# Retention followed by a soft mixture of experts: step 18's keys turned on the chip, one unit of token products held back, the last write in halves

## The chip, the cores and the metric

One Trainium2 chip, one of its cores. The metric is the device time of one execution in microseconds (us), the median of the runs shown. A unit of time in the profile is a us from the start of the profiled span unless it says ns.

## The reference, cut to what matters

```
def _attn_ref(q, k, v):                       # (4, 8, 768, 64) each
    gamma = 1.0 - 2.0 ** (-5.0 - arange(H)); scale = 1.0 / sqrt(D)
    for t in range(S):
        state = gamma * state + einsum('bhd,bhe->bhde', k[:, :, t], v[:, :, t])
        y[:, :, t] = scale * einsum('bhd,bhde->bhe', q[:, :, t], state)

def _moe_ref(x, phi, w1, w2):                 # x (3072, 512), w1 (8, 512, 1024), w2 (8, 1024, 512)
    logits = x @ phi                          # 32 slots, 4 to an expert
    d = softmax(logits over tokens);  slot_input = d.T @ x
    for e in range(E): slot_out[e] = relu(slot_input[e] @ w1[e]) @ w2[e]
    c = softmax(logits over slots);   return c @ slot_out
```

`x` is `y` with its heads beside each other: 4 sequences of 768 tokens, 512 columns.

## The kernel before, in words

Everything is float32. The tokens are cut into 24 **steps** of 128 (4 sequences by 6 chunks, the sequence running fastest), and the steps go in pairs through a loop `for P in range(NPP)` (L451). For each step PE makes scores (`score_mm`, L227), DVE masks them (L235), PE adds the carried state's part and the masked part (L251, L260), sums keys times values into the state (`state_mm`, L288), turns the result back to tokens by rows (`natural_mm`, L304), and the router's logits and dispatch sums follow in groups of four steps. After the loop come two products with the expert weights: `hidden` (L589) with `w1`, and the product with `w2` (L669) in three blocks of output columns, `BLOCKS` = 256, 128 and 128 wide.

**Inputs.** A step's input tile has four parts of 512 columns: keys transposed, queries transposed, values, and the keys once more by tokens (`kn`), which `state_mm` wants as its stationary operand. A step in `TURNED` (L46), and the last four, is "lean": its load (`load_in`, L199) brings 1536 columns, 768 KB, and for a step in `TURNED` PE turns the keys itself (`turn_k`, L206: four 128x128 transposes into a PSUM bank, and one copy by ACT, L207). Any other step loads 2048 columns, 1024 KB (L201). Step `i` is loaded in the iteration `P = (i - 6) / 2` and, when turned, is turned in `P = (i - 2) / 2`, just ahead of that iteration's `natural_mm`. The expert weights are 1 MB tiles (L163, L166) and half tiles (L181), interleaved with the input loads by the table `PACE`.

**Order of the work.** The engines' instructions stand in the order in which the program writes them. All loads and all writes of the output are issued by SP, one queue, in program order, and each has its packets spread over the core's 16 DMA engines, which work through them in that order.

**The end.** When a block's `w2` product is complete in its bank, the generator `finish` (L630) does three things: DVE copies the sums out (`os`, L634); PE repeats the 32 slots over the partitions (`rep`, L638) and DVE copies that (`s4`, L639); then per unit `(m, h)`, 128 output columns by half of the tokens, four **token products** (L650) go into four PSUM banks, are copied by DVE (j even) and ACT (j odd) into an output tile (L655), and SP writes the tile, 768 KB (L656). Blocks 0 and 1 interleave their `finish` with the next block's `w2` product; block 2's has nothing behind it. There are eight units, so eight writes: four of block 0, two of block 1, two of block 2. `rep` is a matrix that repeats the slots; `cT` holds the combine weights; `r` are the ring's 1024-column slots; `b` the 2048-column tiles.

Of the kernel before, what the change touches and what calls it, by code (L numbers as in the profile page):

```python
# [16 lines left out]
B, H, S, D = 4, 8, 768, 64  # L17
C = 128
# [17 lines left out]
BLOCKS = [(0, 256), (256, 128), (384, 128)]  # L36
Y1 = (3, 3, 1)
# [5 lines left out]
NIN = 6  # L43
NRING = 9
PACE = (1, 1, 1, 2, 1, 2, 1, 2, 2, 0, 2, 2)
TURNED = (0, 1, 2, 3, 4, 8, 12, 14)  # L46
SIW = 48
LEAN = [i for i in range(1, NSTEP) if i in TURNED or i >= NSTEP - B]
FULL = [i for i in range(1, NSTEP) if i not in LEAN]
# [32 lines left out]
def retention_soft_moe_kernel(  # L82
# [9 lines left out]
    nc = tc.nc  # L92
# [6 lines left out]
    big = ctx.enter_context(tc.tile_pool(name="big", bufs=NBIG))  # L99
# [18 lines left out]
    rep = small("rep", [128, 128])  # L118
# [7 lines left out]
    cT = small("cT", [128, NGRP, C])  # L126
# [324 lines left out]
    for P in range(NPP):  # L451
        last = P == NPP - 1
# [45 lines left out]
        if P < NPP - B // 2:  # L498
            state_mm(P)
            state_add(P)  # L500
        if 2 * P + 2 in TURNED:
            turn_k(2 * P + 2, "A0")
# [66 lines left out]
    for k in range(NK):  # L569
        nc.tensor.matmul(sp[:, k, :], acc[:, k * 128:(k + 1) * 128], wsel, start=True, stop=True,  # L570
                         skip_group_check=True)
# [51 lines left out]
    load_weights(len(weights))  # L623

    co_tags = ["sm", "A2", "Y1", "A3", "S"]
    last_tags = ["S", "sm", "A2", "Y1", "A3", "A1", "A0", "Y0"]
    pend = []
    n_co = [0]

    def finish(cb, op):  # L630
        c0, w = BLOCKS[cb]
        os_ = small("os", [128, 256])
        s4 = slot()
        nc.vector.tensor_copy(os_[:, :w], op[:, :w])  # L634
        for _ in range(Y1[cb] - 1):
            yield
        rp = bank("Y0")
        nc.tensor.matmul(rp[:, :w], rep, os_[:, :w], start=True, stop=True)  # L638
        nc.vector.tensor_copy(s4[:, :w], rp[:, :w])  # L639
        for _ in range(Y2[cb] - 1):  # L640
            yield
        for m in range(w // 128):
            for h in range(2):
                ot = large(big)[:, 0:12 * C].rearrange("p (c j t) -> p c j t", j=B, t=C)
                cps = []
                for j in range(B):
                    tags = co_tags if cb < len(BLOCKS) - 1 else last_tags
                    cp = bank(tags[n_co[0] % len(tags)]).rearrange("p (c t) -> p c t", t=C)[:, 0:3]
                    n_co[0] += 1
                    nc.tensor.matmul(cp, s4[32 * j:32 * j + 32, m * 128:(m + 1) * 128],  # L650
                                     cT[32 * j:32 * j + 32, 3 * h:3 * h + 3, :], start=True, stop=True,
                                     skip_group_check=True, tile_position=(32 * j, 0))
                    cps.append(cp)
                for j in range(B):
                    (nc.scalar.copy if j % 2 else nc.vector.tensor_copy)(ot[:, :, j, :], cps[j])  # L655
                nc.sync.dma_start(out[c0 + m * 128:c0 + (m + 1) * 128, h * 12 * C:(h + 1) * 12 * C],  # L656
                                  ot.rearrange("p c j t -> p (c j t)"))
                for _ in range(BURST[cb]):
                    yield

    for cb, (c0, w) in enumerate(BLOCKS):
        if cb == len(BLOCKS) - 1:
            n_co[0] = 0
        op = bank(("A0", "A1")[cb % 2])
        units = ([(g, 4 * hf + f) for hf in range(2) for g in range(2) for f in range(4)] if cb == 0 else
                 [(g, fc) for g in range(2) for fc in range(NFC)])
        for n, (g, fc) in enumerate(units):
            for j in range(4):
                nc.tensor.matmul(op[32 * j:32 * j + 32, :w], hT[fc // 4][:, fc % 4, 4 * g + j, :],  # L669
                                 w2t[4 * g + j, cb, fc], start=(n == 0), stop=(n == len(units) - 1),  # L670
                                 skip_group_check=True, tile_position=(0, 32 * j))
            if cb == 0 and n == 2:
                hidden_t(1)
            for f in pend:
                next(f, None)
        done = finish(cb, op)
        next(done)
        for f in pend:
            for _ in f:
                pass  # L680
        pend = [done]
    for _ in pend[0]:
        pass


def lay_out(q, k, v, moe_phi, moe_w1, moe_w2):
# [51 lines left out]
```

## Time and profile before

| | |
|---|---|
| median of 3 runs | 158.61 us (158.42 to 158.70) |
| the profiled execution's own time | 158.41 us |
| its span, first to last instruction | 156.6 us |
| PE busy | 144.6 us, 92% |
| DVE, ACT, POOL busy | 77.8, 42.2, 58.8 us |
| DMA moved | 62.48 MB, 399 GB/s over the span; the hardware queue's packets take 96.6% of 16 engines' span |
| mean granted TensorE clock | 0.984 |

A "share" of DMA is the time that packets took over the time of all 16 engines, so 0.06 is one engine. PE's busy time is modelled and takes pipelined products as one stretch. "Landing" of a DMA is the moment when the last of its 16 engines has reported its part.

### The profile page before, as it was taken

The page shows a single profiled execution, that of the slowest core. Times are in us where ns is not written, and L with a number is a line of the kernel's source. Part 1 is how long each engine was busy: PE and PEld are TensorE (multiplying, and loading weights), DVE is VectorE, ACT ScalarE, POOL GpSimd, SP SyncE. Part 2 cuts the span into 40 slices and gives each one's busy share as a digit, 9 for nine tenths or more (in the row PEclk, how much of TensorE's full clock was granted, in tenths as well). Part 3 has the DMA queues.
Part 4 walks back from the last instruction along what each step waited for, and adds up shares of the span by engine and source line. Part 5 has one row for each costly group of instructions (what it writes and reads, how often), then busy time and mean ns, then how long its engine had stood idle before and what let it go on. Part 6 is the DMA issues. An engine that isn't in the chain of part 4 may idle for free.

```text
span 156.6 us, 5484 instructions
## 1 busy us (share of the span) xinstructions
PE 144.6 (92%) x2412; PEld 107.4 (69%) x2412; DVE 77.8 (50%) x187; ACT 42.2 (27%) x100; POOL 58.8 (38%) x66
## 2 busy tenths in 40 slices
PE   7999999999999999999999979999999999999500
PEld 2688989897988789979996857864232555557200
DVE  0379337682865483768574847566010104535500
ACT  3215422333232316220613042344100001424300
POOL 1351986784936294654938283010000000000000
PEclk9999999999999999999999999999999999999985
DMA  4999999999999999999999999999999999999891
GB/s 159 421 424 421 416 419 416 416 414 419 406 423 408 423 419 410 427 398 431 404 419 412 415 411 416 400 408 421 411 428 416 423 416 416 414 415 417 348 402 78
DMA packets 9816, 62.48 MB, mean 399 GB/s; under 512 B 1088, under 2 KB 1088, under 8 KB 4544
## 3 DMA queue, kind: packets, MB, share of 16 engines
q1 hardware_dynamic: 9792, 62.13, 96.6%
q8 instruction: 19, 0.31, 0.8%
q14 instruction: 5, 0.04, 0.1%
HBM read 55.84 MB, written 6.29 MB: 397 GB/s over the span
## 4 chain that ended last, share of the span: by engine, by line
PE 92%; DVE 2%; issue 1%; DVEq 0%
PE A L227 16%; PE Y L260 15%; PE A L669 9%; PE A L304 7%; PE Y L251 6%; PE S L288 6%; PE Y L589 4%; PE A L589 4%; PE sm L328 4%; PE sm L424 3%; PE S L384 3%; PE A L206 2%; PE sm L650 2%; PE S L650 1%; PE Y L650 1%; PE Y L638 1%
## 5 line engine op out<-in xcount | busy, mean ns | idle before, releaser
L235 DVE TENSOR_TENSOR r<-A,mi 128x512 f32<-128x512 f32 (+1 forms) x50 | 30.1, 662 | 22.1 <-PE A L227 22.1
L212 POOL TENSOR_TENSOR b<-b,qtab 128x512 f32<-128x512 f32 x20 | 25.7, 1287 | 23.5 <-DMA b<-in_x_dram 18.3
L227 PE MATMUL A<-b 64*128 64x128 f32 x384 | 25.4, 280 | 0.0
L227 PEld LDWEIGHTS A<-b 64*128 64x128 f32 x384 | 22.7, 188 | 3.1 <-issue 2.0
L217 POOL TENSOR_TENSOR b<-b,kt 128x512 f32<-128x512 f32 x23 | 23.6, 1046 | 2.4 <-DMA b<-in_x_dram 2.4
L260 PE MATMUL Y<-r,b 128*64 128x128 f32 x352 | 22.5, 276 | 0.5 <-issue 0.5
L260 PEld LDWEIGHTS Y<-r,b 128*64 128x64 f32 x352 | 19.2, 137 | 2.9 <-issue 2.6
L669 PE MATMUL A<-b,r 128*32 128x128 f32 (+1 forms) x336 | 15.9, 300 | 0.0
L311 ACT COPY r<-A 128x512 f32<-128x512 f32 x23 | 12.4, 592 | 8.6 <-PE A L304 8.6
L669 PEld LDWEIGHTS A<-b,r 128*32 128x32 f32 x336 | 10.3, 109 | 6.4 <-issue 4.4
L304 PE MATMUL A<-mi,r 128*128 128x128 f32 x96 | 13.3, 278 | 0.3 <-ACT r L279 0.3
L288 PE MATMUL S<-b 128*64 128x64 f32 x304 | 11.1, 222 | 0.6 <-issue 0.6
L304 PEld LDWEIGHTS A<-mi,r 128*128 128x128 f32 x96 | 10.4, 141 | 1.7 <-ACT r L279 0.5
L288 PEld LDWEIGHTS S<-b 128*64 128x64 f32 x304 | 10.4, 138 | 0.5 <-issue 0.5
L251 PE MATMUL Y<-b,sst 64*64 64x128 f32 x304 | 10.6, 276 | 0.0
L416 POOL TENSOR_TENSOR cn<-cn,cz 128x128 f32<-128x128 f32 x6 | 2.4, 401 | 19.6 <-DVE cz L415 7.2
L280 DVE COPY r<-Y 128x512 f32<-128x512 f32 x9 | 6.2, 690 | 5.9 <-PE Y L260 5.1
L251 PEld LDWEIGHTS Y<-b,sst 64*64 64x64 f32 x304 | 8.2, 132 | 1.2
L328 PEld LDWEIGHTS sm<-r,kt 128*32 128x32 f32 x192 | 6.2, 110 | 3.3 <-issue 3.3
L408 ACT ACTIVATE cn<-cn 128x128 f32<-128x128 f32 x6 | 1.9, 310 | 21.2 <-DVE cn L407 21.2
L328 PE MATMUL sm<-r,kt 128*32 128x128 f32 x192 | 7.4, 273 | 0.0
L297 DVE TENSOR_TENSOR sst<-sst,S 128x256 f32<-128x256 f32 x16 | 6.0, 418 | 2.7 <-PE S L288 2.5
(140 smaller groups left out, 182.9 us busy)
## 6 DMA issues: line engine op xcount, KB each, us to landing
b<-in_w_dram SPq DMA_DIRECT2D x29, 1024.0 KB, 15.1
b<-in_x_dram SPq DMA_DIRECT2D x12, 1024.0 KB, 12.5
b<-in_x_dram SPq DMA_DIRECT2D x11, 768.0 KB, 10.7
out_dram<-b SPq DMA_DIRECT2D x8, 768.0 KB, 8.7
r<-in_w_dram SPq DMA_DIRECT2D x5, 512.0 KB, 11.0
b<-in_first_dram SPq DMA_DIRECT2D x1, 512.0 KB, 3.5
r<-in_first_dram SPq DMA_DIRECT2D x1, 512.0 KB, 4.3
sst<-in_w_dram SPq DMA_DIRECT2D x1, 512.0 KB, 11.7
```

The lines of the kernel that those rows point to most:

```text
L212: nc.gpsimd.tensor_tensor(q, q, qtab, ALU.mult)
L217: nc.gpsimd.tensor_tensor(v, v, vsc[:, i // B, a:b].unsqueeze(2).broadcast_to([128, b - a, D]), ALU.mult)
L227: nc.tensor.matmul(s["sc"][r][:, g, :], s["kT"][half(r), g, :], s["qT"][half(r), g, :], start=True, stop=True, skip_group_check=True)
L235: nc.vector.tensor_tensor(s["A"][:, r, g:g + n], s["sc"][r][:, g:g + n], mask.unsqueeze(1).broadcast_to([128, n, C]), ALU.mult)
L251: nc.tensor.matmul(p["y"][k][b][half(half_of(r, g)), gl, :], sst[(2 * P + k) % B][half(r), g, :], s["qT"][half(r), g, :], start=(gl == 0 a ...
L260: nc.tensor.matmul(pr[P]["y"][k][g // 2][half(half_of(r, g)), g % 2, :], s["v"][:, 2 * g + r, :], s["A"][:, r, g, :], start=(P < B // 2 an ...
L288: nc.tensor.matmul(S_[half(r), k, g, :], s["kn"][:, 2 * g + r, :], s["v"][:, 2 * g + r, :], start=True, stop=True, skip_group_check=True)
L304: nc.tensor.transpose(X[k][:, g * 128:(g + 1) * 128], pr[P]["yT"][:, k, g, :], ident)
L311: (nc.scalar.copy if engines[k] == "scalar" else nc.vector.tensor_copy)(xn, pr[P]["X"][k])
L328: nc.tensor.matmul(q["ltp"][32 * j:32 * j + 32, :], phis[:, p, :], st[GRP * g + j]["yT"][:, p, :], start=(p == 0), stop=(p == NPAIR - 1), ...
L589: nc.tensor.matmul(hp[hf][32 * j:32 * j + 32, :], si0[:, a:a + NSLOT], w1t[hf, g, k][:, j * 512:(j + 1) * 512], start=(g == 0 and k == 0), ...
L669: nc.tensor.matmul(op[32 * j:32 * j + 32, :w], hT[fc // 4][:, fc % 4, 4 * g + j, :], w2t[4 * g + j, cb, fc], start=(n == 0), stop=(n == le ...
```

## The change

Three edits. Step 18 joins `TURNED`, so its keys by tokens are no longer loaded but turned by PE. Block 1's second unit of token products is held back: it is done after block 2's `w2` product and ahead of block 2's own token products. Block 2's last unit is written in two DMAs, token groups j = 0, 1 and j = 2, 3, the first as soon as its two copies are done. The order of PSUM banks for block 2's units is rotated to match, and `finish` is cut into helpers.

```
-TURNED = (0, 1, 2, 3, 4, 8, 12, 14)
+TURNED = (0, 1, 2, 3, 4, 8, 12, 14, 18)
...
-    last_tags = ["S", "sm", "A2", "Y1", "A3", "A1", "A0", "Y0"]
+    last_tags = ["A3", "A1", "A0", "Y0", "S", "sm", "A2", "Y1"]
...
+    def token_store(cb, ot, m, h, j0=0, j1=B):
+        c0 = BLOCKS[cb][0]
+        rows = out[c0 + m * 128:c0 + (m + 1) * 128, h * 12 * C:(h + 1) * 12 * C]
+        nc.sync.dma_start(rows.rearrange("p (c j t) -> p c j t", j=B, t=C)[:, :, j0:j1, :], ot[:, :, j0:j1, :])
...
         for m in range(w // 128):
             for h in range(2):
...
+                if (cb, h) == (NB - 2, 1):
+                    held.append(s4)
+                    return
...
-        done = finish(cb, op)
-        next(done)
+        if cb < NB - 1:
+            done = finish(cb, op)
+            next(done)
...
+    os_ = out_sum(NB - 1, op)
+    cps = token_mm(NB - 2, held[0], 0, 1)
+    rp = out_rep(NB - 1, os_)
+    ot = token_tile()
+    token_copy(ot, cps, (0, 1, 3))
+    s4 = out_slots(NB - 1, rp)
+    token_copy(ot, cps, (2,))
+    token_store(NB - 2, ot, 0, 1)
+    n_co[0] = 0
+    last = []
+    for h in range(2):
+        last.append((token_tile(), token_mm(NB - 1, s4, 0, h)))
+    for h, (ot, cps) in enumerate(last):
+        token_copy(ot, cps, (0, 1))
+        if h == 1:
+            token_store(NB - 1, ot, 0, h, 0, 2)
+        token_copy(ot, cps, (2, 3))
+        token_store(NB - 1, ot, 0, h, 2 * h, B)
```

`out_sum`, `out_rep`, `out_slots`, `token_mm` and `token_copy` hold the lines that stood in `finish`: the copy of the sums, the product with `rep`, its copy, the four token products and their copies. A half of a write takes 2 of 4 token groups, so each of the 128 rows is three pieces of 256 columns.

On SP's queue, the one that carries every transfer, the step loads in the middle and the output's writes at the end read as below, as one difference (`in_x` are the steps, `in_w` the expert weights):

```order
 L201 DMA b<-in_x_dram 128x2048 x2
 L163 DMA b<-in_w_dram 128x2048
-L201 DMA b<-in_x_dram 128x2048 x2
+L199 DMA b<-in_x_dram 128x1536
+L201 DMA b<-in_x_dram 128x2048
 L163 DMA b<-in_w_dram 128x2048 x2
...
 L166 DMA b<-in_w_dram 128x2048 x10
-L656 DMA out_dram<-b 128x1536 x8
+L671 DMA out_dram<-b 128x1536 x7
+L671 DMA out_dram<-b 128x3x256 x2
```

One of the step loads is 512 columns narrower, and the eighth write has become two of 128x3x256.

On PE at the very end, before, from block 1's first unit on (`A_2011` is block 2's bank, the lines with `cT` are token products):

```order
L650 MATMUL A_2042<-cT,r 128x384
L669 MATMUL A_2011<-b,r 32x128 x12
L650 MATMUL S<-cT,r 128x384
L650 MATMUL sm<-cT,r 128x384
L650 MATMUL A_2066<-cT,r 128x384
L650 MATMUL Y_2068<-cT,r 128x384
L669 MATMUL A_2011<-b,r 32x128 x32
L638 MATMUL Y_2110<-os,rep 128x128
L650 MATMUL S<-cT,r 128x384
```

and in the changed kernel:

```order
L655 MATMUL A_2047<-cT,r 128x384
L702 MATMUL A_2016<-b,r 32x128 x44
L655 MATMUL S<-cT,r 128x384
L655 MATMUL sm<-cT,r 128x384
L655 MATMUL A_2105<-cT,r 128x384
L655 MATMUL Y_2107<-cT,r 128x384
L640 MATMUL Y_2109<-os,rep 128x128
L655 MATMUL A_2120<-cT,r 128x384
```

The four token products of block 1's second unit have moved from between the `w2` products to behind the last of them, ahead of the product with `rep`.

## Rows read from the trace of the kernel before

**Rows 1.** The page of the profiled execution: span, PE's busy time, the DMA totals and the hardware queue.
```profile
span 156.6 us, 5484 instructions
PE 144.6 (92%) x2412; PEld 107.4 (69%) x2412; DVE 77.8 (50%) x187; ACT 42.2 (27%) x100; POOL 58.8 (38%) x66
...
DMA packets 9816, 62.48 MB, mean 399 GB/s; under 512 B 1088, under 2 KB 1088, under 8 KB 4544
...
q1 hardware_dynamic: 9792, 62.13, 96.6%
```

**Rows 2.** The page's DMA issues: out<-in, queue, count, KB of each, median us from issue to landing.
```profile
b<-in_x_dram SPq DMA_DIRECT2D x12, 1024.0 KB, 12.5
b<-in_x_dram SPq DMA_DIRECT2D x11, 768.0 KB, 10.7
...
b<-in_first_dram SPq DMA_DIRECT2D x1, 512.0 KB, 3.5
```

**Rows 3.** Windows of 1 us at the end: busy time of PE, PEld, DVE, ACT and POOL with their instructions, granted clock, DMA share, GB/s.
```profile
146.00:147.00 1.00, 0.77 (x12) 0.54 (x15) 0.18 (x1) 0.00 (x0) 0.00 (x0) 1.00 0.99 412
147.00:148.00 1.00, 0.80 (x12) 0.19 (x4) 0.82 (x2) 0.78 (x3) 0.00 (x0) 1.00 0.70 281
148.00:149.00 1.00, 0.00 (x0) 0.00 (x0) 1.00 (x3) 0.84 (x3) 0.00 (x0) 1.00 0.55 221
149.00:150.00 1.00, 0.00 (x0) 0.00 (x0) 0.13 (x1) 0.00 (x0) 0.00 (x0) 1.00 0.96 399
...
152.00:153.00 1.00, 0.00 (x0) 0.00 (x0) 0.00 (x0) 0.00 (x0) 0.00 (x0) 0.50 0.90 369
153.00:154.00 1.00, 0.00 (x0) 0.00 (x0) 0.00 (x0) 0.00 (x0) 0.00 (x0) 0.50 0.33 135
154.00:155.00 1.00, 0.00 (x0) 0.00 (x0) 0.00 (x0) 0.00 (x0) 0.00 (x0) 0.50 0.18 74
```

**Rows 4.** The output's line L656, one write at a time by a window around its issue (the sixth, seventh and eighth): duration of the issue in ns, its start, and the us from issue to landing.
```profile
L656 SPq DMA_DIRECT2D out_dram<-b x1: 332/332/332, 143.8 to 143.8; - x1
...
DMA to landing us min/median/max: 8.0/8.0/8.0
...
L656 SPq DMA_DIRECT2D out_dram<-b x1: 333/333/333, 148.3 to 148.3; - x1
...
DMA to landing us min/median/max: 5.4/5.4/5.4
...
L656 SPq DMA_DIRECT2D out_dram<-b x1: 332/332/332, 149.2 to 149.2; - x1
...
DMA to landing us min/median/max: 6.3/6.3/6.3
```

**Rows 5.** The DMA view of three windows: 114 to 130, where all data packets but one are of 8 KiB; 143 to 146, where all are of 6 KiB and are writes of the output; and 97 to 110, of 4 and 8 KiB. Packets, MB, then the hardware queue's packets, MB and share of 16 engines.
```profile
DMA packets 914, 6.70 MB, mean 419 GB/s; under 512 B 97, under 2 KB 97, under 8 KB 97
...
q1 hardware_dynamic: 913, 6.69, 100.7%
...
DMA packets 230, 1.27 MB, mean 422 GB/s; under 512 B 24, under 2 KB 24, under 8 KB 230
...
q1 hardware_dynamic: 230, 1.27, 101.6%
...
DMA packets 1062, 5.35 MB, mean 411 GB/s; under 512 B 118, under 2 KB 118, under 8 KB 703
...
q1 hardware_dynamic: 1060, 5.32, 100.8%
```

**Rows 6.** The chain of waits around the ends of the iterations P = 6 (which turns step 14) and P = 8 (which turns nothing): start, us, engine, what it writes, line.
```profile
59.88 0.59 PE A L206 x4
60.46 0.87 PE A L304 x8
61.34 0.11 PE sm L364
61.44 1.99 PE A L227 x32
...
76.08 1.02 PE A L304 x8
```

**Rows 7.** The chain of waits at the end, from the middle of block 2 on; x64 is the last run of its `w2` products.
```profile
141.06 0.79 PE A L669 x24
141.85 0.52 PE S L650
...
143.06 1.93 PE A L669 x64
...
146.23 0.58 PE S L650
...
148.66 0.46 DVE b L655
```

**Rows 8.** The timeline of DVE at the end: start, us, line, what it writes, shapes, count, and idle time before with what ended it.
```profile
145.01 0.29 DVE L634 COPY os<-A 128x128 f32<-128x128 f32 x1 [1.26 <-PE A L669]
...
145.88 0.29 DVE L639 COPY r<-Y 128x128 f32<-128x128 f32 x1 [0.58 <-PE Y L638]
...
147.18 0.56 DVE L655 COPY b<-S 128x384 f32<-128x384 f32 x1 [1.00 <-PE Y L650]
...
147.65 1.48 DVE L655 COPY b<-A 128x384 f32<-128x384 f32 x3
```

More of the change, by code (lines that the diff above doesn't have):

```diff
@@ L625, in retention_soft_moe_kernel, with out_sum, out_rep, out_slots @@
     co_tags = ["sm", "A2", "Y1", "A3", "S"]
-    last_tags = ["S", "sm", "A2", "Y1", "A3", "A1", "A0", "Y0"]
+    last_tags = ["A3", "A1", "A0", "Y0", "S", "sm", "A2", "Y1"]
     pend = []
     n_co = [0]
+    NB = len(BLOCKS)
+    def out_sum(cb, op):
+        w = BLOCKS[cb][1]
+        os_ = small("os", [128, 256])
+        nc.vector.tensor_copy(os_[:, :w], op[:, :w])
+        return os_
+    def out_rep(cb, os_):
+        w = BLOCKS[cb][1]
+        rp = bank("Y0")
+        nc.tensor.matmul(rp[:, :w], rep, os_[:, :w], start=True, stop=True)
+        return rp
+    def out_slots(cb, rp):
+        w = BLOCKS[cb][1]
+        s4 = slot()
+        nc.vector.tensor_copy(s4[:, :w], rp[:, :w])
+        return s4
+    def token_mm(cb, s4, m, h):
+        tags = co_tags if cb < NB - 1 else last_tags
+        cps = []
+        for j in range(B):
+            cp = bank(tags[n_co[0] % len(tags)]).rearrange("p (c t) -> p c t", t=C)[:, 0:3]
+            n_co[0] += 1
+            nc.tensor.matmul(cp, s4[32 * j:32 * j + 32, m * 128:(m + 1) * 128],
+                             cT[32 * j:32 * j + 32, 3 * h:3 * h + 3, :], start=True, stop=True,
+                             skip_group_check=True, tile_position=(32 * j, 0))
+            cps.append(cp)
+        return cps
+    def token_tile():
+        return large(big)[:, 0:12 * C].rearrange("p (c j t) -> p c j t", j=B, t=C)
+    def token_copy(ot, cps, js):
+        for j in js:
+            (nc.scalar.copy if j % 2 else nc.vector.tensor_copy)(ot[:, :, j, :], cps[j])
+    def token_store(cb, ot, m, h, j0=0, j1=B):
+        c0 = BLOCKS[cb][0]
+        rows = out[c0 + m * 128:c0 + (m + 1) * 128, h * 12 * C:(h + 1) * 12 * C]
+        nc.sync.dma_start(rows.rearrange("p (c j t) -> p c j t", j=B, t=C)[:, :, j0:j1, :], ot[:, :, j0:j1, :])
     def finish(cb, op):
[L631 to L634, printed above, removed]
+        w = BLOCKS[cb][1]
+        os_ = out_sum(cb, op)
         for _ in range(Y1[cb] - 1):
             yield
-        rp = bank("Y0")
-        nc.tensor.matmul(rp[:, :w], rep, os_[:, :w], start=True, stop=True)
-        nc.vector.tensor_copy(s4[:, :w], rp[:, :w])
+        s4 = out_slots(cb, out_rep(cb, os_))
         for _ in range(Y2[cb] - 1):
@@ L643, in finish @@
             for h in range(2):
[L644 to L657, printed above, removed]
+                if (cb, h) == (NB - 2, 1):
+                    held.append(s4)
+                    return
+                cps = token_mm(cb, s4, m, h)
+                ot = token_tile()
+                token_copy(ot, cps, range(B))
+                token_store(cb, ot, m, h)
                 for _ in range(BURST[cb]):
                     yield
+    held = []
     for cb, (c0, w) in enumerate(BLOCKS):
-        if cb == len(BLOCKS) - 1:
+        if cb == NB - 1:
             n_co[0] = 0
@@ L681, in retention_soft_moe_kernel @@
         pend = [done]
-    for _ in pend[0]:
-        pass
+    os_ = out_sum(NB - 1, op)
+    cps = token_mm(NB - 2, held[0], 0, 1)
+    rp = out_rep(NB - 1, os_)
+    ot = token_tile()
+    token_copy(ot, cps, (0, 1, 3))
[12 more added lines that the diff above has]
+        token_store(NB - 1, ot, 0, h, 2 * h, B)
 def lay_out(q, k, v, moe_phi, moe_w1, moe_w2):
```

## The prediction, made before the changed kernel was run

> **What bounds the kernel now.** The page first: PE is busy 92% of the span, and the DMA engines carry 62.48 MB with the hardware queue's packets taking 96.6% of 16 engines' time [rows 1]. Two resources are nearly full, so the question is which of them sets the end. The chain of waits runs on PE nearly all the way and stops at DVE's last copy, 148.66 + 0.46 = 149.1 [rows 7]. But the span is 156.6 [rows 1]. The last 7.5 us hold no compute at all; they are the output's writes. So look at the writes one by one: the sixth lands at 143.8 + 8.0 = 151.8, the seventh at 148.3 + 5.4 = 153.7, the eighth at 149.2 + 6.3 = 155.5 [rows 4]. They are issued 4.5 and 0.9 us apart and land 1.9 and 1.8 us apart. A write of 768 KB is 128 packets of 6 KiB, 8 to an engine; at 237 ns each (below) that is 1.9 us. So whichever engine lands last goes from one write into the next with no pause, and the time at which a write was issued doesn't show in its landing.
>
> The windows tell which engines these are [rows 3]. From 147 to 149 the share falls to 0.70 and 0.55: some engines had nothing left, because the seventh write was not yet issued. From 149 all are at it again. Then the share falls to 0.33 in 153 to 154 and 0.18 in 154 to 155: 0.18 of 16 is three engines. Three engines are about 1.8 us behind the rest, were never out of work at 147 to 149, and end the kernel. What they have to move, and not PE, sets the time. A microsecond of PE at the end is worth nothing until those three run dry.
>
> How long can they be fed late? A write issued to idle engines starts after about 0.9 us (issued at 148.3, the share is back at 149.0 to 149.3), and it lands about 0.4 us after its last packets. On the three late engines the fifth write lands about 1.9 before the sixth, at 149.9, so its data end near 149.5, and the sixth write is in time if issued by 148.6. It is issued at 143.8: slack of almost 5 us. The eighth has nearly 3.
>
> **The change, part by part.** *Fewer bytes.* One step's load becomes 768 KB instead of 1024 KB, as for the eleven lean ones [rows 2]: on each engine 8 packets of 6 KiB in place of 8 of 8 KiB. Prices [rows 5]: in 114 to 130 the queue's 913 - 97 = 816 data packets of 8 KiB take 1.007 x 16 x 16 us, so 315.9 ns each; in 143 to 146, 206 packets of 6 KiB take 1.016 x 16 x 3 us, 236.7 ns each (each with its share of completion marks). 8 x (315.9 - 236.7) = **-0.63 us** on every engine, the three late ones included. I take 6 KiB writes as the price of 6 KiB reads; the byte rates, 422 and 419 GB/s, leave little room.
>
> *Four transposes and a copy.* In P = 6 the transposes are 0.59 and `natural_mm` 0.87; in P = 8, without them, it is 1.02 [rows 6]. So PE gets 0.59 - 0.15 = +0.44 us later from P = 8 on, with the scores following without a gap (61.34 + 0.11 to 61.44), so ACT's copy out of the bank hides under `natural_mm`. Behind PE stand the loads that wait for free tiles; they come 0.44 later while the queue is 0.63 ahead. A load lands 10 us or more after its issue in the median [rows 2], so 1.1 us less lead leaves the engines fed. Cost on the end: 0. If the lead were gone it would be 0.44.
>
> *The held unit.* Block 1's second token products sit between `w2` products: from 141.85 to 143.06, 1.21 us of PE's chain [rows 7]. Without them the last `w2` product ends at 144.99 + 0.44 - 1.21 = 144.2. The held products start there. From product to copy takes 0.95 (146.23 to 147.18) [rows 7, 8], so DVE copies j = 0 at 145.2 to 145.7. The product with `rep` now queues behind four token products on PE, about 0.5 us; the sums' copy to the slots' copy was 145.01 to 145.88, so the latter comes at 144.3 + 0.87 + 0.5 = 145.7, and ends at 146.0; j = 2 then takes 0.5 and the held write is issued at **146.6**, 2.8 later than now. Every write behind it on SP waits for it. It has to be there by 148.6 - 0.6 = 148.0. Margin 1.4: cost 0. The last block's products start at 146.0, copies at 147.0, DVE's four take about 2 us (0.56 + 1.48 now): writes at 148.1, 148.5 and 149.1, against 148.3 and 149.2 now, and wanted at about 150 and later. The other engines idle longer from 145 on and finish nearer to the late three, which costs nothing while they stay ahead.
>
> *The halves.* A row of a half is three pieces of 1 KiB, so the last write is 768 packets instead of 128: 48 to an engine. No row has a 1 KiB packet, so I bound it. Below: the byte rate of 6 KiB, 39.4 ns, which adds 0. Above: the window of 4 and 8 KiB packets [rows 5] has 1060 - 703 = 357 of 8 KiB and 703 - 118 = 585 of 4 KiB in 1.008 x 16 x 13 = 209.7 us; less 357 x 315.9 ns, a 4 KiB packet takes 165.6 ns. A line through 4 and 8 KiB gives 52.9 ns at 1 KiB, which adds 48 x 52.9 - 1894 = +0.65; through the steepest pair, 4 and 6 KiB, 59 ns and +0.94. Below nothing I see no way: the bytes are the same. I take 43.6 ns, a third of the way to the line, **+0.20 us**, since the row nearest in kind is the writes' and it has no overhead over 8 KiB. The second half's earlier issue gains nothing, as the queue isn't empty.
>
> The Trainium skill, DMA: Bandwidth & Descriptors, section Why small descriptors are slow, has a fixed cost of about 3 cycles for a packet of 32-byte beats; by its 850 MHz, my estimate from the page is 48 x 35 against 8 x 195 cycles, +0.14 us, and the sum would be -0.49. No row here shows it.
>
> **Sum:** -0.63 + 0 + 0 + 0.20 = -0.43 us. The profiled execution, 158.41 with a span of 156.6, would be 157.98 with 156.2; it is 0.2 under the median of 158.61. From the median: **158.18 us**.
>
> **The rivals.** *The pieces cost what the bytes save.* At 52.6 ns a piece (48 x 52.6 = 1894 + 630) nothing is left, and the line through 4 and 8 KiB gives just that: 158.3 to 158.9 for 46 to 59 ns. For it: 4 KiB packets do show an overhead. Against: 6 KiB writes don't.
>
> *PE sets the end after all.* The page's 92% and the chain speak for it. Then the saved bytes are worth nothing, the last issue moves by -0.1, and the time is 158.5. The landings speak against it.
>
> *Slower: the pieces are dearer than any line here.* Place: the last write on the three late engines. It decides from 52.6 ns on; at half the byte rate, 79 ns, it is 48 x 79 - 1894 = +1.9, and the time 158.61 - 0.63 + 1.9 = 159.9. For it: they are a sixth of anything this trace moved. Against: from 8 to 4 KiB the price rose by little.
>
> *The three run dry.* If the held write is issued after 148.0, each us is a us on the end; at 149.5 the sum is -0.43 + 1.5 and the time 159.7. It needs my tail to be 1.4 us too short, with every step of it read from a row.
>
> *A transfer has a fixed cost of its own.* A lone 512 KB load takes 3.5 us [rows 2], 8 x 165.6 ns = 1.3 of it data; if the other 2.2 stood in the queue, the ninth write would add them: 160.4. The eight writes land 1.8 to 1.9 apart, all of it data, so it overlaps. The Trainium skill, DMA: Bandwidth & Descriptors, section Rules for kernel authors, speaks for one large transfer over many small ones, which is this rival's side; the trace agrees only for a lone one.
>
> **How the numbers follow.** A measurement tells about 0.2%, 0.32 us, from no change, so faster means under 158.29. The forecast with a piece up to 46 ns, 157.98 to 158.29, gets 0.58. Pieces that give the gain back, and PE at the end, get 0.13 each: same 0.26. The dear pieces get 0.10, the dry engines 0.04, the fixed cost 0.02: slower 0.16. The range runs from the free pieces less 0.13 of scatter, 157.85, up through the give-back cases, 158.85; what it leaves out is the slower ones.
>
> **What the changed profile would show.** Right: loads after step 18 land 0.6 earlier; landings of full writes 1.8 to 1.9 apart; the held write issued near 146.6; a last stretch with about three engines busy; the two halves together landing 2.0 to 2.2 after the write before; span 156.2. Wrong: a share of zero on the late engines before the held write; halves landing 2.6 or more after; a span moved by what PE moved.

## The result, and the profile after

The change makes the kernel slower: 159.99 us against 158.66 in the same sessions (medians of 8 runs each), a ratio of 1.0074, 95% interval 1.0054 to 1.0093. A ratio, here and below, is worked out from all the single runs, so it is not the quotient of the two medians. The forecast was 158.18. The profiled execution took 160.05 with a span of 158.3, 1.7 more than that of before. The page's head, to be held against [rows 1]:

```profile
span 158.3 us, 5498 instructions
PE 144.9 (92%) x2416; PEld 107.7 (68%) x2416; DVE 79.7 (50%) x187; ACT 42.5 (27%) x101; POOL 58.5 (37%) x66
...
DMA packets 10472, 62.22 MB, mean 393 GB/s; under 512 B 1104, under 2 KB 1872, under 8 KB 5328
...
q1 hardware_dynamic: 10448, 61.87, 95.9%
q8 instruction: 19, 0.31, 0.8%
```

The edit did what it says: 0.26 MB fewer, four more products on PE, more and smaller packets. PE's busy time rose by 0.3, the span by 1.7. Note the last row: the same row stands in the page of before, and the prediction passed it over. The tail is where the time is. The windows of the end, in the columns of [rows 3]:

```profile
148.00:149.00 1.00, 0.52 (x8) 0.47 (x12) 0.80 (x3) 0.48 (x2) 0.00 (x0) 1.00 0.34 141
149.00:150.00 1.00, 1.00 (x16) 0.34 (x8) 0.60 (x2) 0.56 (x2) 0.00 (x0) 1.00 0.47 182
150.00:151.00 1.00, 0.05 (x4) 0.00 (x0) 1.00 (x3) 1.00 (x3) 0.00 (x0) 1.00 0.99 399
...
155.00:156.00 1.00, 0.00 (x0) 0.00 (x0) 0.00 (x0) 0.00 (x0) 0.00 (x0) 0.50 0.84 300
156.00:157.00 1.00, 0.00 (x0) 0.00 (x0) 0.00 (x0) 0.00 (x0) 0.00 (x0) 0.50 0.07 24
```

```profile
149.00:149.50 0.50, 0.50 (x12) 0.34 (x8) 0.10 (x1) 0.06 (x1) 0.00 (x0) 1.00 0.06 25
149.50:150.00 0.50, 0.50 (x8) 0.00 (x0) 0.50 (x2) 0.50 (x2) 0.00 (x0) 1.00 0.88 340
```

Before, some engines idled at 147 to 149 and three never did. Now the share is 0.06 from 149.0 to 149.5, one engine of 16 on average, and from 149.4 to 149.7 no packet of data is under way: all of them ran dry, the three late ones too. And at the very end one engine works alone for a us (0.07). Among what the engines move from 149 to 154 is one transfer of the queue q8, 1.4% of 16 engines for 5 us, so 1.1 us of one:

```profile
q8 instruction: 1, 0.02, 1.4%
```

It starts at 149.75, together with the held write. The DMA view from 149.60 to 149.85, in which the write's packets begin (the first at 149.69) and none has ended, so that each is another engine's:

```profile
q1 hardware_dynamic: 15, 0.09, 89.2%
q8 instruction: 1, 0.02, 27.5%
```

Fifteen engines begin the write and the sixteenth moves instructions. By the trace's packets never more than 15 packets of data are under way until the transfer ends at 150.85, and 16 from then on.

The writes, as in [rows 4]: the fifth and the sixth, which is the held one.

```profile
L671 SPq DMA_DIRECT2D out_dram<-b x1: 332/332/332, 144.0 to 144.0; - x1
DMA to landing us min/median/max: 5.7/5.7/5.7
...
L671 SPq DMA_DIRECT2D out_dram<-b x1: 332/332/332, 148.9 to 148.9; - x1
DMA to landing us min/median/max: 4.8/4.8/4.8
```

The fifth lands at 149.7, the held one at 153.7, the seventh (issued at 150.5, landing 5.0 later) at 155.5. Writes that follow each other without a pause land 1.8 to 1.9 apart, so 2.1 us were lost between the fifth and the sixth, and none behind it. The trace marks the landing on each engine: fifteen have landed the held write by 152.1 and one at 153.6; the last half is landed by fifteen at 156.3 and by one at 157.3. Why was the held write issued at 148.9 and not at 146.6? The chain at the end, against [rows 7]:

```profile
141.26 0.79 PE A L702 x24
...
142.91 2.09 PE A L702 x68
145.00 0.85 issue
145.85 0.85 PE A L702 x20
...
147.56 0.43 PE Y L640 x2
```

Two causes. In the last run of `w2` products PE stands still for 0.85 us in the middle of 88 products, with "issue" as the reason: no engine's result was missing. And PE arrives late: block 1's first unit starts at 141.26 + 0.79 = 142.05. In the chain of before it stands behind this row, at 140.20, so PE is 1.85 late, and 0.44 of that was forecast:

```profile
139.41 0.79 PE A L669 x24
```

### The profile page after: what moved, and what is told of

It is laid out like the page before. It is cut to its first block, busy times and chain, and to the rows that moved or that the text cites. A ratio compares the mean times of both kernels' runs of the same rounds, so it can differ in the third digit from the quotient of the medians.

```text
span 158.3 us, 5498 instructions
## 1 busy us (share of the span) xinstructions
PE 144.9 (92%) x2416; PEld 107.7 (68%) x2416; DVE 79.7 (50%) x187; ACT 42.5 (27%) x101; POOL 58.5 (37%) x66
## 4 chain that ended last, share of the span: by engine, by line
PE 83%; DMA 5%; DVE 4%; issue 2%; ACT 1%; SPq 1%; DVEq 0%; ACTq 0%
PE A L227 13%; PE Y L260 12%; PE A L702 9%; PE A L304 7%; PE S L288 6%; PE Y L251 6%; DMA b<-in_x_dram 5%; PE Y L589 4%; PE A L589 4%; PE sm L328 4%; PE S L384 3%; PE A L206 2%; DVE r L235 2%; PE sm L655 2%; PE S L655 1%
## 5 line engine op out<-in xcount | busy, mean ns | idle before, releaser
L260 PE MATMUL Y<-r,b 128*64 128x128 f32 x352 | 22.5, 277 | 0.7 <-issue 0.7
L260 PEld LDWEIGHTS Y<-r,b 128*64 128x64 f32 x352 | 19.1, 137 | 3.2 <-issue 2.9
L304 PE MATMUL A<-mi,r 128*128 128x128 f32 x96 | 13.3, 278 | 0.8 <-ACT r L279 0.7
L288 PE MATMUL S<-b 128*64 128x64 f32 x304 | 11.1, 222 | 1.0 <-issue 1.0
L304 PEld LDWEIGHTS A<-mi,r 128*128 128x128 f32 x96 | 10.5, 141 | 2.1 <-ACT r L279 1.1
L288 PEld LDWEIGHTS S<-b 128*64 128x64 f32 x304 | 10.4, 138 | 0.6 <-issue 0.6
L408 ACT ACTIVATE cn<-cn 128x128 f32<-128x128 f32 x6 | 1.9, 310 | 22.8 <-DVE cn L407 22.8
L655 PE MATMUL A<-cT,r 32*128 32x384 f32 x26 | 7.1, 528 | 0.5 <-ACT b L666 0.5
```

Of the source, the lines that this page charges most:

```text
L260: nc.tensor.matmul(pr[P]["y"][k][g // 2][half(half_of(r, g)), g % 2, :], s["v"][:, 2 * g + r, :], s["A"][:, r, g, :], start=(P < B // 2 an ...
L288: nc.tensor.matmul(S_[half(r), k, g, :], s["kn"][:, 2 * g + r, :], s["v"][:, 2 * g + r, :], start=True, stop=True, skip_group_check=True)
L304: nc.tensor.transpose(X[k][:, g * 128:(g + 1) * 128], pr[P]["yT"][:, k, g, :], ident)
```

## The experiments

Theory 1: step 18 makes PE late, the held write is late with it, and the DMA engines run dry (the forecast's small rival). Theory 2, which came up with the traces: PE's own instructions travel as 16 KB transfers (q8, 19 of them, 0.31 MB), on the same DMA engines and in PE's way. Ratios are to the kernel before in the same session, with the 95% interval.

### Each part by itself

Step 18's edit alone, in the kernel before:

```
-TURNED = (0, 1, 2, 3, 4, 8, 12, 14)
+TURNED = (0, 1, 2, 3, 4, 8, 12, 14, 18)
```

> Only step 18 joins the turned ones; no unit held, last write whole. Theory A (the lead is spent: PE comes 1.0 to 1.9 us later, the DMA engines run dry near 92, and the held write, which hangs on PE, then comes too late for the late engines): without a held write the late engines keep most of their lead, 158.0 to 158.7. Theory B (the 1 KiB pieces cost the time): 158.0. Theory C (PE sets the end by itself): later by what PE is late, 159.6 or more.

Measured: 159.25 against 158.57, 1.0032 [1.0011, 1.0053].

The held unit alone: the changed kernel with step 18 out of `TURNED` and the last write whole:

```
-        token_copy(ot, cps, (0, 1))
-        if h == 1:
-            token_store(NB - 1, ot, 0, h, 0, 2)
-        token_copy(ot, cps, (2, 3))
-        token_store(NB - 1, ot, 0, h, 2 * h, B)
+        token_copy(ot, cps, range(B))
+        token_store(NB - 1, ot, 0, h)
```

> Only the held unit, step 18 loaded in full, last write whole. Theory A: PE is not late in the loop, so the held write is issued near 147.5 and in time for the late engines; 158.5 to 158.9, and up to 159.4 if PE's last instruction fetch falls on an engine that then has no slack. Theory B: 158.6. Theory C: PE's tail is up to 1 us longer, 159.0 to 159.6.

Measured: 158.82, 1.0018 [1.0002, 1.0035].

The halves alone, in the kernel before (`cut` is true for block 2's last unit):

```
+                    if cut and j % 2:
+                        nc.sync.dma_start(rows.rearrange("p (c j t) -> p c j t", j=B, t=C)[:, :, j - 1:j + 1, :],
+                                          ot[:, :, j - 1:j + 1, :])
```

> Only the last write in halves of 1 KiB pieces. Theory A: the two halves take 0.1 to 0.4 us longer than the whole, 158.7 to 159.0. Theory B: the whole loss is here, 159.7 to 160.3. Theory C: no change or a little faster, 158.2 to 158.6.

Measured: 158.77, 1.0016 [1.0000, 1.0033]. So no part gains by itself, and step 18's edit loses most.

Step 18's bytes alone: the narrow load, no transposes. It leaves out the turning: step 18's state is summed from the columns of the transposed keys as they lie.

```
-    LEAN = [i for i in range(1, NSTEP) if i in TURNED or
+    LEAN = [i for i in range(1, NSTEP) if i in TURNED + (18,) or
...
+            if i == 18:
+                st[i]["kn"] = t[:, 0:512].rearrange("p (h d) -> p h d", d=D)
```

> Step 18's keys by tokens are not loaded and not turned either: the state takes the 512 columns of the transposed keys in their place, so that part of the result is left out. The bytes alone, no work on PE or ACT. Theory A and B, where the late DMA engines set the end: 0.6 us faster, 158.0. Theory C: no change, 158.6, since PE does what it did. If the earlier data shift other engines against each other (a DVE subtraction that took 1.3 us beside GpSimd in the changed kernel), PE is late by 0.5 here too, and it shows in the chain near 66.

Measured: 158.56, 1.0002 [0.9978, 1.0026]. The interval leaves a gain of 0.35 us at the most, not 0.63. And the work alone, with the full load:

```
-        if 2 * P + 2 in TURNED:
+        if 2 * P + 2 in TURNED + (18,):
```

> The kernel before, with step 18's keys both loaded in full and turned on PE: PE's part of the edit without the bytes. Transposes on the path (theory): P = 8's stretch 0.4 to 0.55 us longer, PE 0.5 to 1.0 late at the end, yet the writes' late engines still end the kernel and the eighth write is no more than 0.5 late, so 158.7 to 159.2, ratio 1.001 to 1.004, like the kernel with both parts of the step's edit (1.0032). Rival, bytes saved ahead of the gated weight loads do count: this one is 0.6 slower than the kernel with both parts, 159.8 or more, ratio 1.007 and up. Second rival, PE's lateness costs nothing: 158.6, ratio 1.000.

Measured: 159.00 against 158.74, 1.0017 [1.0002, 1.0032]. The rival that the bytes count and this one is worse by them is out.

Are bytes then worthless? The last expert-weight load brings 1536 of its 2048 columns, the missing products take an earlier block (that part of the result is not computed):

```
+            if not weights:
+                nc.sync.dma_start(t[:, 0:1536], w2[w2n[0], :, 0:1536])
```

> The kernel before, with 256 KB fewer in the very last load of expert weights (four of its blocks stand in for the four left out, so that part of the result is left out); the same work on all engines. Theory A, now put so: the late DMA engines do set the end, but bytes saved before about 92 are spent there, where the next load waits for PE to free a tile and engines that are ahead run dry; bytes saved behind that place count in full: 0.6 us faster, 158.0. Theory C (what the DMA engines carry doesn't set the end): no change, 158.6, as in the run that saved step 18's bytes alone.

Measured: 157.93 against 158.68, 0.9960 [0.9939, 0.9982], so -0.63 us by the ratio (0.29 to 0.97). That agrees with the price the forecast put on 256 KB. Late bytes count in full; step 18's don't. Between the two lies a gate. The windows of before and then of the changed kernel at 92 to 95:

```profile
92.00:93.00 1.00, 0.69 (x6) 0.21 (x3) 0.69 (x1) 0.45 (x1) 1.00 (x1) 1.00 1.03 426
93.00:94.00 1.00, 0.97 (x9) 0.80 (x9) 0.00 (x0) 0.49 (x2) 1.00 (x2) 1.00 1.05 401
94.00:95.00 1.00, 1.00 (x19) 1.00 (x20) 0.16 (x1) 0.75 (x3) 1.00 (x2) 1.00 1.07 434
```

```profile
92.00:93.00 1.00, 0.67 (x12) 0.67 (x14) 0.77 (x4) 0.28 (x2) 1.00 (x2) 1.00 0.75 311
93.00:94.00 1.00, 1.00 (x19) 0.83 (x15) 0.00 (x0) 0.69 (x4) 1.00 (x2) 1.00 0.47 180
94.00:95.00 1.00, 0.64 (x4) 0.33 (x4) 0.69 (x1) 0.26 (x1) 0.77 (x2) 1.00 0.82 197
```

The changed kernel's engines lose 0.25 + 0.53 + 0.18, about 1 us of 16 engines, there. What they wait for is one weight load (L163), which on SP waits for PE to free its tile; the waits of SP at 80 to 96, and the load's issue and landing, in the changed kernel:

```profile
SPq L163 <- PE Y L260: 7.6, 1, 7.6
```

```profile
L163 SPq DMA_DIRECT2D b<-in_w_dram x1: 327/327/327, 93.3 to 93.3; - x1
DMA to landing us min/median/max: 5.7/5.7/5.7
```

In before it is issued at 91.4 and lands 7.8 later. Engines that are ahead by saved bytes reach this load before PE lets it start. The bytes-alone kernel has the dip too, 0.77, 0.80 and 0.85 in the same three windows. It issues this load at 92.6, 1.2 later than before, though PE turns nothing more there; so PE's lateness in the loop is not the transposes' alone.

### The parts in pairs

The changed kernel with step 18 out of `TURNED`, so the held unit and the halves:

> The change without its first edit: the held unit and the halves, step 18 loaded in full. If the three edits add up as they did alone (held +0.28, halves +0.25 us), 159.1. If the held write's lateness and the halves meet on the same engines and one eats the other's slack, up to 159.6. If step 18 is what loses the time, 158.6.

Measured: 158.78 against 158.68, 1.0008 [0.9991, 1.0025].

The changed kernel with the last write whole (the diff above), so step 18 and the held unit:

> The change without its third edit: step 18 turned and the unit held, the last write whole. Adding up (+0.5 and +0.28 us): 159.4. If the halves are the main loss beside them: 158.8. If the late PE makes the held write late (the sixth write issued after 148.6 and all engines dry before it), 159.6 or more.

Measured: 160.28, 1.0092 [1.0063, 1.0122], with the sixth write issued at 149.1, behind the 148.6 of the last branch. So the loss lies between step 18 and the held unit. To test lateness alone, the unit is moved less far, in the kernel before with step 18's edit and the halves:

```
-BURST = (3, 3, 3)
+BURST = (3, 7, 3)
```

> Step 18's edit and the halves, and block 1's second unit neither held nor where it stood, but four twelfths of a block later: behind the 14th of the 16 runs of four products, so that its write is issued 1 to 1.5 us later than before and 2 or more ahead of the changed kernel's. Theory (each us that the sixth write comes behind the late engines' need is a us of the end, and short of that it is free): the sixth write at about 146, ahead of the need, 158.8 to 159.3, ratio 1.001 to 1.004, about the sum of step 18's edit and the halves alone (+0.5 and +0.25). Rival, step 18 and any move of this unit lose by PE's longer chain in itself: 159.8 to 160.3, ratio 1.007 to 1.010.

Measured: 159.17 against 158.74, 1.0029 [1.0012, 1.0046], with the sixth write issued at 146.5. As the theory had it: about the sum of the two parts alone, and no more.

### PE's instruction stream

The "issue" stall in the last `w2` products has an odd place. The chain in the kernel without step 18, and in the changed kernel with eight products fewer on PE (its diff stands below):

```profile
141.23 2.10 PE A L702 x72
143.33 0.79 issue
```

```profile
142.36 2.31 PE A L702 x76
144.67 0.67 issue
```

After 68 products with all of the change, after 72 where PE's stream is four products shorter, after 76 where it is eight shorter. The stall sits at one instruction number of the stream, whatever the instruction does, so PE waits there for its own instructions. The other kernels with the held unit agree: after 68 in all five with as long a stream as the change, after 72 in both that are four products shorter. In these eight profiles a transfer of q8 starts ahead of the stall (at 143.3 in the changed kernel), and the stall ends 2.4 to 2.6 us behind its start. The ninth has no stall: there the transfer started at 141.4, and 2.5 us on PE had not yet come to product 76. The Trainium skill, Advanced Engine Details and Errata, section ISA Cache, gives a cache line of 16 KB, 256 instructions. For 2416 products of a weight load and a multiplication each, my estimate from the page is 4832 / 256 = 18.9 such lines; the trace agrees, with 19 transfers of 0.31 MB in all. The stall falls into the last `w2` run, where products are short and, with the unit held, 88 come in a row; before, the longer token products broke that run, and no such stall stands there. That PE gets ahead of its transfers because the run is unbroken is my reading of this; no run tests it.

One kernel puts products behind the end of the changed program, to move the last transfer:

```
+    warm(7, "A3", 512)
```

> The changed kernel with seven products of 512 columns with a constant behind PE's last token product, nothing else. In the changed kernel a 16 KB transfer of PE's own instructions started at 149.8, when PE came to its end, and one DMA engine was 1.0 to 1.5 us behind the other 15 from then on. If that transfer makes the end, PE's end moves to about 156, the transfer falls behind the writes, and the time is 0.7 to 1.0 us less: 159.0 to 159.3. If it doesn't matter: 160.0; if PE's extra work itself delays the end: over 160.3.

Measured: 160.43, 1.0113 [1.0083, 1.0142]. The last transfer stayed ahead of the end, at 150.5, so it decides nothing about what it was made for. Its held write was issued at 150.0, 1.1 later than in the changed kernel, though nothing ahead of it had been edited.

The next shortens the stream at its start (the short stream, below). `warm` issues products whose result nobody reads; half as many of twice the width take the same PE time:

```
-WARM = 4
+WARM = 2
-WN = 256
+WN = 512
...
-    warm(2, "A0", 128)
+    warm(1, "A0", 256)
```

> The whole change, with the warm-up products merged into half as many of twice the width: the same PE time and 10 to 16 fewer instructions in PE's stream, so the last of the queue of PE's own instruction transfers should come at the end of the program or not at all. Theory A, the loss over 159.0 is that last transfer, which sets one engine 1.0 to 1.5 us behind when all stand level: 158.8 to 159.3, ratio 1.001 to 1.004, and the held write's 16 engines land within 0.3 us. Theory B, the loss is the late held write by itself: 159.8 to 160.3, ratio 1.007 to 1.010, however the transfers fall.

Measured: 158.42 against 158.74, 0.9987 [0.9966, 1.0009]: by the ratios 1.4 us less than the whole change, with all its parts in, and below the ranges of both theories. Its page has one transfer fewer inside the span, and its end, in the columns of the windows:

```profile
q8 instruction: 18, 0.29, 0.8%
```

```profile
149.00:150.00 1.00, 0.33 (x5) 0.00 (x0) 1.00 (x3) 1.00 (x4) 0.00 (x0) 1.00 0.98 412
...
155.00:156.00 1.00, 0.00 (x0) 0.00 (x0) 0.00 (x0) 0.00 (x0) 0.00 (x0) 0.50 0.17 57
```

All engines end within 155 to 156; no single one trails by a us. But the held write was issued at 148.1, 0.7 earlier than in the changed kernel, so theory B's late write wasn't as late here. Is it the shape of the warm-up? Cut the first of it again, so that the stream is as long as the change's:

```
-    warm(WARM)
+    warm(4, "sm", 128)
+    warm(2, "sm", 256)
```

> The kernel with merged warm-up products, with the first of them cut in narrower pieces so that PE's stream has as many instructions as the whole change again, at the same PE time. Theory A (the last transfer of PE's instructions, at 149 to 150 with all engines level, costs 1 to 1.5 us): the transfer is back at about 149, one engine ends 1.0 to 1.5 us behind the other 15, 159.6 to 160.2, ratio 1.006 to 1.010. Rival (the merged warm-up gained by its shape): 158.3 to 158.7, ratio 0.998 to 1.000, like the kernel with fewer instructions.

Measured: 1.0108 [1.0074, 1.0142]. The same kernel again:

> The put-back kernel once more, for a profile at full clock: the merged warm-up with its first part cut, as many instructions as the whole change. Theory A: the last instruction transfer at 149 to 151, one engine's part of the held write 1.0 to 1.5 us after the others', ratio 1.007 to 1.012. Rival (its loss comes from PE alone): all parts of the held write within 0.4 us and the loss in PE's stalls.

Measured: 160.57 against 158.64, 1.0094 [1.0063, 1.0125]. The transfers of instructions between 149 and 154, the chain's stall, and a window of the end:

```profile
q8 instruction: 1, 0.02, 1.1%
```

```profile
144.07 2.09 PE A L703 x68
146.16 0.89 issue
```

```profile
157.00:158.00 1.00, 0.00 (x0) 0.00 (x0) 0.00 (x0) 0.00 (x0) 0.00 (x0) 0.50 0.10 33
```

The last transfer is back, the stall is back at 68, and so is the trailing engine. The transfer holds 1.1% of 16 engines for 5 us, 0.9 us on one engine; one engine lands the held write 0.9 behind the others, a little less than theory A's 1.0 to 1.5, and the last half 0.5 behind them, at 158.0. The other fifteen end at 157.5, where the kernel with the short stream ends at 155.7: most of the difference is PE, whose held write was issued at 150.1 and not at 148.1. So the length of the stream moves PE and the transfer together. Now the length without step 18's work, by the same cut in the kernel of the held unit and the halves:

> The held unit and the halves without step 18, and four more warm-up products in the same time, so that PE's stream has the length of the whole change without its work in the loop. Theory A in its strong form (the transfer alone): it falls at about 148, and 159.5 to 160, ratio 1.005 to 1.008. The form that I hold (the transfer costs only where it hits an engine that isn't ahead any more; the held write is here issued near 147, before the late engines are dry): 0.2 to 0.8 over the same kernel without it (1.0008), so 158.9 to 159.5, ratio 1.002 to 1.006. Rival, late PE alone: 158.7, ratio 1.000 to 1.001.

Measured: 160.00 against 158.84, 1.0058 [1.0026, 1.0089], where 1.0008 stood without the four products. That is the upper half of what was expected. Step 18's work isn't needed for the loss. But a premise failed: the held write was issued at 148.2 and not near 147 (146.9 without the four products). And in the profile the transfer can be charged with 0.2 us at the most: fourteen engines end by 155.9 and two trail, at 156.8 and 157.0, and the one transfer of that stretch, at 151.3, can lie on only one of the two. One engine had landed the fifth write as late as 151.1 already, against 150.1 with the short stream.

Step 18 and the held unit, the last write whole, with the short stream:

> Step 18 and the held unit with merged warm-up products and the last write whole. All 16 engines end level, so each of the halves costs its pieces on all of them: a whole write took 1.83 to 1.9 us and two halves 2.2. So 0.3 to 0.4 less than with halves: 158.0 to 158.2, ratio 0.995 to 0.997. Rival, the halves cost nothing (between the kernels of the whole change they were 0.3 the other way, inside the scatter): 158.4, ratio 0.998 to 1.000.

Measured: 158.86 against 158.84, 0.9994 [0.9970, 1.0017], where 1.0092 stood with the long one. That it would beat the halved version was wrong.

All kernels with the held unit, then, by the number of instruction transfers that their page counts in the span, with the start of the held write's issue:

| held unit with | transfers | held write issued at | ratio |
|---|---|---|---|
| nothing else | 18 | 147.4 | 1.0018 |
| halves | 18 | 146.9 | 1.0008 |
| step 18, short stream | 18 | 146.7 | 0.9994 |
| step 18, halves, short stream | 18 | 148.1 | 0.9987 |
| halves, four products more | 19 | 148.2 | 1.0058 |
| step 18, halves (the change) | 19 | 148.9 | 1.0074 |
| step 18 | 19 | 149.1 | 1.0092 |
| step 18, halves, put back (two sessions; the time is the second's) | 19 | 150.1 | 1.0108, 1.0094 |
| step 18, halves, products at the end | 19 | 150.0 | 1.0113 |

The ratios of the two groups lie apart, up to 1.0018 and from 1.0058, though the intervals of the nearest two kernels still overlap (1.0002 to 1.0035 and 1.0026 to 1.0089). Step 18 is on both sides of the line, and so are the halves. But the third column parts the groups at the same line, so the table can't tell the transfer from a late write. PE's stalls in the loop (L288 and L260) grow with the stream as well: 0.9 and 1.2 us in the two with the short stream, 1.2 and 1.9 in the two first rows, 1.7 to 2.1 in the other five. What tells them apart is the profiles. Up to 148.2 the last engine lands each write without a pause behind the one before, 1.8 to 2.1 apart. From 148.9 on the engines run dry first, all of them in three profiles and all but two or so in the put-back kernel's. In each of these four, 15 packets of data are under way at most while the transfer runs, and 16 as soon as it has ended.

Two controls without the held unit. The kernel before with the short stream (the same diff of `warm`):

> The kernel before with merged warm-up products, 16 instructions fewer on PE. If the merged warm-up gains by its shape, 157.2 to 157.9, ratio 0.991 to 0.995. If it is the transfer: the last one, at 147.6 in the kernel before, goes behind the end; it hits one of three late engines there, and the other two stay late, so 158.3 to 158.7, ratio 0.997 to 1.000.

Measured: 158.41 against 158.84, 0.9975 [0.9956, 0.9994]. It beats the kernel before. But the last transfer did not go behind the end, it stayed at 19, so the reason given for the size was wrong. Its PE stalls are shorter, 0.8 us against 1.1; that this is the cause isn't shown.

And the same with step 18's edit:

> The kernel before with step 18's edit and the merged warm-up: no held unit, the last write whole. If step 18 loses only by the transfer that its longer stream brings in: ratio 0.995 to 0.999, near the kernel before with merged warm-up (0.9975). If its later PE costs by itself, 0.4 to 0.5 over that one: 1.000 to 1.002.

Measured: 159.00, 1.0011 [0.9991, 1.0031], again with 19 transfers, and 0.36% over the one without step 18. So step 18 costs about what it cost in the long stream (0.32%): its own price, apart from the transfer.

### A wait of ACT

In half of the profiles PE waits 0.4 us longer near 68, behind an exponent on ACT (L408) that waits for a DVE copy. Its call is moved an iteration on, in the kernel before:

```
+        if P % 2 == 1 and g > 0:
+            combine_a(g - 1)
...
-        if P % 2 == 0 and P > 0:
+        if P == NPP - 2:
```

> The kernel before, with the combine weights' exponent (ACT, which waits for a DVE copy) issued in the next iteration, behind the copy that PE's next products wait for. Theory: the 0.45 us that PE waits near 68 us in half of the profiles (PE A L304 behind ACT's copy) cannot come any more; as that wait doesn't stand in the profile of before, the time moves by 0 to -0.3: 158.3 to 158.7, ratio 0.998 to 1.001. Rival, the wait was in most of the runs that had no profile: 158.0 to 158.3, ratio 0.996 to 0.998. Rival, the later exponent is late for the token products: over 159, ratio 1.003 and up.

Measured: 158.82 against 158.74, 1.0012 [0.9994, 1.0030]. The wait was not removed: among PE's waits L304 still waits 0.8 us for ACT at one place, and L384 now waits 1.8 us for DVE.

## Why the prediction was wrong, step by step

**What bounds the kernel** was right. The end is the landing of the writes on late DMA engines: 256 KB less on them gave the forecast price. By the marks of landing the three were 1.4 us behind the rest, not 1.8.

**Fewer bytes, -0.63: the first failed step.** The price was right, as far as its interval tells, and the place wrong. "1.1 us less lead leaves the engines fed" took the median of all loads from issue to landing. The load that counts, L163 at 91.4, had 7.8, stands behind a wait for PE, and came 1.9 later. Bytes saved ahead of it were waited away: 1.0002 for the bytes alone.

**Transposes and copy, 0: the second.** Their own length was right, 0.59 + 0.87 in P = 8 against 1.02, with these rows of P = 8 for [rows 6]:

```profile
77.07 0.59 PE A L206 x4
77.66 0.87 PE A L304 x8
```

But PE was 1.85 late at block 1's units and not 0.44, and it did cost: 0.17% with the bytes loaded, 0.32% with them saved. The waits of PE in the whole run, of before and then of the changed kernel:

```profile
PE S L288 <- issue: 0.6, 2, 0.3
PE Y L260 <- issue: 0.5, 1, 0.5
...
PE A L304 <- ACT r L279: 0.3, 1, 0.3
```

```profile
PE S L288 <- issue: 1.0, 2, 0.5
PE A L702 <- issue: 0.9, 1, 0.9
...
PE Y L260 <- issue: 0.7, 1, 0.7
PE A L304 <- ACT r L279: 0.7, 2, 0.5
...
PE A L227 <- DMA b<-in_x_dram: 0.2, 1, 0.2
```

Ahead of the tail that is 0.4 + 0.2 + 0.4 + 0.2 = 1.2 of the 1.4 that the forecast lacked. Of these, the wait on ACT and the one on the first load also come and go between kernels that share the edit, so they are scatter of timing; stalls on instructions are longer in the changed kernel's loop, as in the other kernels with the long stream, and the trace doesn't say why.

**The held unit, 0 with a margin of 1.4: the step that decided.** The write was issued at 148.9 instead of 146.6: 1.4 brought from the loop and 0.85 from the stall at product 68. It was wanted by 148.0, so the rival "the three run dry", given a chance of 0.04, is what happened: 0.06 of DMA share at 149.0 to 149.5. That rival's own rule, each us late is a us, gives 0.9 of the 2.1 lost. The landings give less to lateness: fifteen engines land the held write 2.4 behind the fifth's last landing, so about 0.6 is lost by the late write, and the sixteenth loses 1.5 more. For that no step had a term: it is the engine on which the last instruction transfer lies, at 149.75 to 150.85, when all engines stand level and none has a lead to spend on it, and it trails to the end. At the end fifteen engines are 0.8 behind the end of before (156.3 against 155.5) and the sixteenth is 1.0 behind these. The held unit let all engines run dry, and so made them level; the 88 short products in a row, on which PE waits for its instructions, made it later still. The runs on the stream's length (0.9987 to 1.0094, 1.0008 to 1.0058) don't single out the transfer, as the held write came later in both, by 1.9 and 1.3; its part is read from the profiles of the four kernels whose write came at 148.9 or later.

**The halves, +0.20.** Alone they took 0.16%, 0.25 us, as forecast within the interval. The DMA view of the changed kernel from 154.2 to 155.2, almost all of it their packets:

```profile
DMA packets 341, 0.35 MB, mean 348 GB/s; under 512 B 16, under 2 KB 338, under 8 KB 341
...
q1 hardware_dynamic: 341, 0.35, 98.8%
```

16 us x 0.988 less 3 packets of 6 KiB at 0.237 is 15.1, by 338 - 16 = 322 pieces 46.9 ns each, with their marks; 43.6 was taken (a third of the way from 39.4 to 52.9 is 43.9, which changes the sum by 0.01). On 48 pieces to an engine that is +0.36 instead of +0.20, with all 16 engines busy. Where the late ones work nearly alone, as the forecast had it, its figure holds: in the kernel of the halves alone the seventh and the last landing, 153.79 and 155.81, are 2.02 apart, against 1.84 before. On the trailing engine of the changed kernel they are 1.89 apart, so the halves cost its end 0.05. The estimate of +0.14 from the Trainium skill (DMA: Bandwidth & Descriptors, Why small descriptors are slow) is under the forecast's figure and near the +0.18; the measurement decides. The dear-pieces rival (from 52.6) and the fixed cost are out: the last half lands 1.9 after the seventh write, at 151.4 + 5.9 = 157.3, where the trailing engine works alone. The landings of the two halves in the changed kernel, as one row:

```profile
DMA to landing us min/median/max: 5.4/5.7/5.9
```

**PE sets the end** is out for the kernel before, where late bytes moved the time by what they weigh, with the same work on PE. In the changed kernel PE comes in through the held write: it sets when the dry engines start again.

**What stays open.** The split of the loss at the end, 0.8 on fifteen engines and 1.0 more on the one with the transfer, is that of one profiled run. Two of the changed kernel's eight runs took only 158.9 and 159.2, and no trace says what was different in them. Why the stalls in the loop grow with the stream, and why the short stream helps the kernel before, too. And whether the halves cost the whole change anything: the pairs (0.0074 to 0.0092, 0.9987 to 0.9994) point the other way, inside their intervals.

## What to carry to other kernels

A saved byte is worth its price only behind the last point at which the transfers wait for compute; ahead of it, look up the one load that stands in a queue behind a wait, not the median of all. Where a tail is to be made tight by letting all engines end level, every small transfer in it goes straight to the end, and the engines' own instructions are such transfers: count them on the page, and look where the last one falls. A margin is to be held against what the timing scatters between kernels (here more than 1 us on PE), not against the edit's own cost alone.

## What the runs showed of the hardware that was not expected

- PE's instructions come in 16 KB transfers over the DMA engines (19, 0.31 MB, 0.8% of their time), and PE stops when it reaches instructions that haven't come: 0.2 to 1.1 us at a time, at one number of the stream, 2.6 us in all in the changed kernel.
- Eight products more or fewer at the start of the program, at equal PE time, moved the whole by 1.7 us by the ratios (0.9987 to 1.0094), in the two profiles mostly through PE's later held write (148.1 to 150.1), and the rest through one engine that trails.
- A stretch in which all engines run dry takes away the lead that single engines had: behind it fifteen of the 16 land the held write within 0.2 us of each other, where before three landed the last write 1.4 us behind the rest. A single 16 KB transfer of instructions then sets one engine 1.5 us behind.
